# Six weight conversions in place, and at other places of the slot loop, in a fused attention, expert and MLP kernel

## The chip, the cores and the metric

One core of one Trainium2 chip runs the whole program. The metric is the device time of one execution in microseconds (us).

## What is computed

Three layers follow one another. The reference, cut to its arithmetic:

```python
def phi(x):                                       # q, k, v: (4, 8, 576, 64)
    proj = einsum('bhsd,df->bhsf', x, w_phi)      # 64 -> 128 features
    proj = proj - max(abs(proj), axis=-1)
    return concatenate([exp(proj), exp(-proj)])
num = phi(q) @ (phi(k).T @ v); den = phi(q) @ sum(phi(k)) + 1e-6
x = (num / den)                                   # -> (2304, 512)
e = argmax(normalised x @ normalised expert_emb.T / tau)      # one of 8 experts a token
x = gate * (relu(x @ w1[e]) @ w2[e])              # w1 512x1024, w2 1024x512
h = x @ w_in                                      # w_in 512x2048
out = (h / (1 + exp(-h))) @ w_out                 # w_out 2048x512
```

`w_in` and `w_out` come as 64-bit floats. The kernel reads them as pairs of 32-bit words, low word and high word, and makes 32-bit floats of them with bit operations.

## The kernel before

**The stages.** The attention runs first, batch by batch. The expert stage follows: the tokens are sorted by expert into slots of 128 tokens, and the loop over s handles slots 0 to 21. Last comes the MLP, in Strassen products. A 32-bit product is made of three matmuls of rounded parts (high by high, low by high, high by low), so each operand is split first: ScalarE (ACT) casts the high part, VectorE (DVE) subtracts to get the low part.

**One slot.** In slot s TensorE (PE) does `mm1(s, k)`, k = 0 to 3: 24 matmuls of tokens by w1. Then come four transposes of the next slot's tokens (`xturn(s + 1)`), `mm2(s - 1, i)`, i = 0 to 3: 24 matmuls of the hidden rows of the slot before by w2, and eight transposes of this slot's hidden rows (`hturn(s)`). Beside them run the splits: `split(s + 1, 1, k)` after `mm1(s, k)` and `split(s, 2, i)` after `mm2(s - 1, i)`. A split of a weight quarter is a cast on ACT (L848, raw to wh) and a subtraction on DVE (L849, raw and wh to wl). `halves` does the same for transposed tokens (xh, xl) and hidden rows (hh, hl), with its cast at L853 and its subtraction at L856. The third matmul of each product (L801) reads xl or hl.

**The weights.** `raw1` and `raw2` are two buffers each, one by parity of the slot. SyncE (SP) loads them at L812, in two parts: `load1(s + 3, (0,))` and `load1(s + 2, (1,))` in mm2 of slot s, `load2(s + 1, (0,))` and `load2(s, (1,))` at the head of slot s. A load waits until the splits that read the buffer's old contents are done, and it is left out where the expert does not change. All of SP's transfers are in one queue, in order.

**GpSimd (POOL)** issues its own transfers, in program order: a gather of tokens in each slot (L834), accumulating copies `add_weights` inside a scratch array of w_in blocks in DRAM (L194, by the list WHEN), the raw loads of the conversions (`cload`, L169), and the stores of their results (`keep_weights`, L182 to L186).

**The conversions.** The sixteen 128-wide blocks of w_in are converted one after another: ten in the attention, six, called conversion 0 to 5 here (i = CA to CA + 5 in the code), in the slots. Each is a shift of the low words (DVE; L209 for even i, L212 for odd), a multiplication of the high words by 2^-112 (ACT, L202), a shift-and-or (DVE, L217) and a sign xor (DVE, L219); an odd one adds its two column halves (DVE, L225). All work lies in one tile of the attention that is free by then, named x in the profile. It has 2560 words a partition: two raw halves of 1024 words for even and odd i, and one result buffer of 512 words that all six share (L943, words 2048 to 2560). `convert(s, n)` is called after each split of mm1 (n = k) and of mm2 (n = 4 + i), and the table HOOKS says at which of these places a conversion takes its next of five steps; the fifth stores it. Conversion 0 is in slots 4 and 5, 1 in 6 and 7, 2 in 7 and 8, 3 in 13 and 14, 4 in 14 and 15, 5 in 15 and 16. At the first step of conversion i the raw load of i + 1 is issued.

Of the kernel before, what the change touches and what calls it, by code (L numbers as in the profile page):

```python
# [66 lines left out]
def moe_kernel(ctx, tc, qk, v, w_phi, emb, tau, w1, w2, win, wout, out):  # L67
# [103 lines left out]
    def keep_weights(i, c, rw, dma=nc.sync):  # L171
# [25 lines left out]
    def narrow(rw, c, eng, i):  # L197
        minus = i < NJ and i % 2 == 0
        lo, hi = rw[:, :, 0], rw[:, :, 1]
        def scale():  # L200
            if eng is nc.scalar:
                nc.scalar.mul(out=c.bitcast(F32), in_=hi.bitcast(F32), mul=2.0 ** -112)  # L202
            else:
                eng.tensor_scalar(out=c.bitcast(F32), in0=hi.bitcast(F32), scalar1=2.0 ** -112, scalar2=None,
                                  op0=ALU.mult)

        def shift():
            if minus:
                nc.vector.tensor_scalar(out=lo, in0=lo, scalar1=29, scalar2=-2147483648, op0=ALU.logical_shift_right,  # L209
                                        op1=ALU.bitwise_or)  # L210
            else:
                nc.vector.tensor_scalar(out=lo, in0=lo, scalar1=29, scalar2=None, op0=ALU.logical_shift_right)  # L212

        for f in (shift, scale) if eng is nc.scalar else (scale, shift):
            f()
            yield
# [41 lines left out]
    def phase_all(ctx):  # L258
# [1364 lines left out]
```

## Time and profile before

| | |
|---|---|
| median of three runs | 923.42 us (923.1 to 924.58) |
| the profiled execution's own time | 923.77 us |
| its span in the trace | 922.1 us, so 1.67 us lie outside |
| busy in the span | PE 901.1, DVE 619.6, ACT 581.9, POOL 260.6 us |
| granted clock of PE | 1.00 in all windows that are shown (its upper level, 2.4 GHz) |
| slots 2 to 15 in the trace | 257.29 to 441.59 us |

The profile shows one execution. In a table by windows each line is one stretch of time, with the busy time of every engine in it. In a timeline each line is one instruction or a run of like instructions on one engine, with start and length; a bracket at its end says how long the engine sat idle before it and which instruction or transfer ended that. Names with an arrow are result and operands. SPq is a DMA issue on SP's queue.

### The profile page before, as it was taken

The numbers are of one execution on the slowest core, as the hardware profiler recorded it, in microseconds if no ns is written. First come the engines' busy times: TensorE is split into PE (matmuls) and PEld (weight loads), VectorE is DVE, ScalarE is ACT, GpSimd is POOL, SyncE is SP. The second block draws the span as 40 slices with busy tenths as digits, with TensorE's granted clock in tenths as the row PEclk, the third lists the DMA queues.
The fourth block names the chain that finished last, engine by engine and source line by source line (L and its number), as shares of the span: only waits on it lengthen the run. The fifth ranks groups of instructions, "written<-read, shape, count | busy, mean of one in ns | idle before, by whom it ended". The sixth has DMA issues, their size and how long they took to land. (4 is left out here: it accounts for less than half of the span.)

```text
span 922.1 us, 15645 instructions
## 1 busy us (share of the span) xinstructions
PE 901.1 (98%) x5567; PEld 786.3 (85%) x5567; DVE 619.6 (67%) x967; ACT 581.9 (63%) x948; POOL 260.6 (28%) x236
## 2 busy tenths in 40 slices
PE   8999999999999989999999999999999999999996
PEld 6999999988767767877888799999999888888885
DVE  7888888986798999969989857676756122222220
ACT  6877878745977869869888665343456344444331
POOL 6887877712221434313210020101000100000000
PEclk9999999999999999999999999999999999999999
DMA  6355363349496795793698585877776744444420
GB/s 181 107 152 180 93 178 97 99 126 359 160 256 194 237 240 170 277 322 110 180 335 305 196 289 180 248 248 231 242 255 210 202 115 125 115 114 115 116 67 23
DMA packets 136739, 171.69 MB, mean 186 GB/s; under 512 B 34664, under 2 KB 97768, under 8 KB 136656
## 3 DMA queue, kind: packets, MB, share of 16 engines
q1 hardware_dynamic: 124064, 144.06, 49.4%
q0 software_dynamic: 12512, 26.55, 10.8%
q8 instruction: 45, 0.74, 0.3%
q14 instruction: 38, 0.31, 0.1%
q10 hardware_dynamic: 80, 0.03, 0.0%
HBM read 170.87 MB, written 52.04 MB: 242 GB/s over the span
## 5 line engine op out<-in xcount | busy, mean ns | idle before, releaser
L849 DVE TENSOR_TENSOR wl<-raw,wh 128x1024 fp32r<-128x1024 f32 (+1 forms) x166 | 187.6, 1173 | 28.1 <-ACT wh L848 22.6
L848 ACT CAST wh<-raw 128x1024 fp32r<-128x1024 f32 (+1 forms) x166 | 161.2, 1033 | 22.2 <-PE ph L801 10.8
L1173 DVE TENSOR_TENSOR hlt<-gt,hlt 128x1024 fp32r<-128x1024 f32 x34 | 41.7, 1226 | 146.4 <-ACT hlt L1172 146.4
L1097 ACT COPY ht<-puA 128x288 f32<-128x288 f32 x128 | 50.9, 400 | 91.9 <-PE puA L801 78.9
L800 PE MATMUL po<-wob,hlt 128*128 128x512 f32 x272 | 108.6, 399 | 0.0
L799 PE MATMUL po<-wob,hlt 128*128 128x512 f32 x272 | 107.2, 394 | 0.0
L801 PE MATMUL po<-wob,hlt 128*128 128x512 f32 x272 | 106.6, 392 | 0.0
L435 POOL TENSOR_TENSOR kl<-ke,kh 128x640 fp32r<-128x640 f32 x52 | 84.0, 1636 | 31.0 <-issue 23.1
L1193 ACT COPY os<-po 128x512 f32<-128x512 f32 x17 | 10.0, 587 | 108.0 <-PE po L801 108.0
L485 PE MATMUL pnx<-kv,qp 128*128 128x73 f32 x640 | 76.6, 275 | 0.0
L485 PEld LDWEIGHTS pnx<-kv,qp 128*128 128x128 f32 x640 | 74.1, 192 | 0.1
L1194 POOL DMA_INDIRECT out<-os,oidx x18 | 17.5, 974 | 179.1 <-ACT os L1193 168.6
L799 PE MATMUL ph<-wh,xh 128*128 128x512 f32 x166 | 67.1, 404 | 0.0
L801 PE MATMUL ph<-wh,xl 128*128 128x512 f32 x166 | 65.3, 394 | 0.9 <-DVE xl L856 0.9
L800 PE MATMUL ph<-wl,xh 128*128 128x512 f32 x166 | 64.8, 390 | 0.0
L396 DVE TENSOR_REDUCE m<-pqk 128x10 f32<-128x1280 f32 x32 | 47.5, 1486 | 24.5 <-PE pqk L390 24.5
L1104 DVE TENSOR_TENSOR ht<-puC,ht 128x288 f32<-128x288 f32 x64 | 29.1, 454 | 51.4 <-PE puC L801 44.6
L799 PEld LDWEIGHTS po<-wob,hlt 128*128 128x128 f32 x272 | 51.1, 188 | 13.1
L420 ACT ACTIVATE ke<-d 128x640 f32<-128x640 f32 x52 | 38.3, 737 | 37.0 <-DVE d L397 37.0
L801 PEld LDWEIGHTS po<-wob,hlt 128*128 128x128 f32 x272 | 51.1, 188 | 12.3
L800 PEld LDWEIGHTS po<-wob,hlt 128*128 128x128 f32 x272 | 51.1, 188 | 11.8
L390 PE MATMUL pqk<-wbd,zh 128*128 128x256 f32 (+1 forms) x320 | 59.5, 285 | 0.8 <-DVE d L397 0.6
(403 smaller groups left out, 2438.3 us busy)
## 6 DMA issues: line engine op xcount, KB each, us to landing
raw<-w SPq DMA_DIRECT2D x44, 1536.0 KB
raw<-w SPq DMA_DIRECT2D x44, 512.0 KB
hd<-ht SPq DMA_DIRECT2D x124, 144.0 KB
gt<-hd SPq DMA_DIRECT2D x15, 1024.0 KB
z<-qk SPq DMA_DIRECT2D x32, 288.0 KB
wo<-wout SPq DMA_DIRECT2D x16, 512.0 KB
yd<-ys SPq DMA_DIRECT2D x23, 256.0 KB
raw<-win SPq DMA_DIRECT2D x10, 512.0 KB
```

The lines of the kernel that those rows point to most:

```text
L390: nc.tensor.matmul(out=pqk[0:r, c * 256:(c + 1) * 256], lhsT=z[:, c * P:c * P + r], rhs=wbd[:, j].rearrange("p h f -> p (h f)"), start=(i ...
L396: nc.vector.tensor_reduce(out=m, in_=pv, axis=AX.X, op=ALU.max, apply_absolute_value=True)
L420: nc.scalar.activation(out=ke, in_=kd, func=AF.Exp, scale=1.0 - 2.0 * s)
L435: nc.gpsimd.tensor_tensor(out=kl[:, :, s, :], in0=st.pop(("ke", g, s)), in1=kh[:, :, s, :].bitcast(F32), op=ALU.subtract)
L485: nc.tensor.matmul(out=pn[:, c, 0:73], lhsT=qp[:, s, c * P:(c + 1) * P], rhs=kv[:, s, 0:73], start=(s == 0), stop=(s == 1))
L799: nc.tensor.matmul(out=o, lhsT=ah, rhs=bh, start=first, stop=False, skip_group_check=more)
L800: nc.tensor.matmul(out=o, lhsT=ah, rhs=bl, start=False, stop=False, skip_group_check=more)
L801: nc.tensor.matmul(out=o, lhsT=al, rhs=bh, start=False, stop=last, skip_group_check=more)
L848: nc.scalar.copy(out=hi[:, 0:n], in_=sl[:, 0:n])
L849: nc.vector.tensor_tensor(out=lo[:, 0:n], in0=sl[:, 0:n], in1=hi[:, 0:n].bitcast(F32), op=ALU.subtract)
L1097: nc.scalar.copy(out=htile(u, at), in_=BK[u, "A"])
L1173: nc.vector.tensor_tensor(out=lo, in0=g, in1=hi.bitcast(F32), op=ALU.subtract)
```

## The change

A conversion writes its result back into its own raw half, and the shared buffer is gone. The order of the operations changes with that: shift of the low words, sign xor into the low words, multiplication of the high words in place, then shift-and-or into words 0 to 512 of the half; an odd conversion adds its halves into words 512 to 768 of the same half in that same step. So there are four steps, and loads and stores have tables of their own. The steps are in slots 2 (conversion 0), 7 and 8 (1), 9 (2), 10 (3), 14 (4) and 15 (5). The number of instructions on each engine and the transfers are the same as before; the conversions in the attention and those of w_out keep their operations.

```diff
+    def narrow_in_place(flat, i):
+        rw = flat.rearrange("p (f t) -> p f t", t=2)
+        lo, hi = rw[:, :, 0], rw[:, :, 1]
+        shift(lo, i)
+        yield
+        nc.vector.scalar_tensor_tensor(out=lo, in0=hi, scalar=-2147483648, in1=lo, op0=ALU.bitwise_and,
+                                       op1=ALU.bitwise_xor)
+        yield
+        nc.scalar.mul(out=hi.bitcast(F32), in_=hi.bitcast(F32), mul=2.0 ** -112)
+        yield
+        c = flat[:, 0:512]
+        nc.vector.scalar_tensor_tensor(out=c, in0=hi, scalar=3, in1=lo, op0=ALU.logical_shift_left, op1=ALU.bitwise_or)
+        if i % 2:
             a, b = c.bitcast(F32)[:, 0:256], c.bitcast(F32)[:, 256:512]
-            both = rw.rearrange("p f t -> p (f t)")[:, 0:256].bitcast(F32)
-            nc.vector.tensor_tensor(out=both, in0=a, in1=b, op=ALU.add)
+            nc.vector.tensor_tensor(out=flat[:, 512:768].bitcast(F32), in0=a, in1=b, op=ALU.add)
...
         def cload(i):
             scr = st[B - 1][1].rearrange("p c f -> p (c f)")
-            o = i % 2 * 1024
-            J[i] = [scr[:, o:o + 1024].bitcast(I32).rearrange("p (f t) -> p f t", t=2),
-                    scr[:, 2048:2560].bitcast(I32)]
-            fetch_raw(i, J[i][0], nc.gpsimd)
+            flat = scr[:, i % 2 * 1024:i % 2 * 1024 + 1024].bitcast(I32)
+            J[i] = [flat[:, 0:512], flat[:, 512:768], narrow_in_place(flat, i)]
+            fetch_raw(i, flat.rearrange("p (f t) -> p f t", t=2), nc.gpsimd)
...
-        HOOKS = [(s, n) for s, hs in {4: (1, 5), 5: (1, 5, 7), 6: (1, 3, 5, 7), 7: (1, 3, 5, 7), 8: (1, 3),
-                                      13: (1, 3, 5, 7), 14: (1, 3, 5, 7), 15: (1, 3, 5, 7), 16: (1, 3, 5)}.items()
-                 for n in hs]
-        assert len(HOOKS) == 5 * (NJ - CA)
+        LOADS = {(3, 5): 2, (8, 7): 3, (13, 5): 4, (13, 7): 5}
+        STORES = {(3, 1): 0, (8, 3): 1, (13, 1): 2, (13, 3): 3, (15, 1): 4, (16, 1): 5}
+        STEPS = [(2, (1, 3, 5, 7)), (7, (1, 5, 7)), (8, (1,))] + [(s, (1, 3, 5, 7)) for s in (9, 10, 14, 15)]
+        STEPS = [(s, n) for s, ns in STEPS for n in ns]
```

On ACT, the piece of slot 7 with the multiplication of a conversion, before (conversion 2), with the semaphores that each row waits for:

```order
L848 CAST wh_4356<-raw_1_159 128x1024 [waits DMAHW7_49,DVE_49,PE_49]
L848 CAST wh_4386<-raw_1_159 128x1024 [waits DVE_49,PE_49]
L202 ACTIVATE x<-x 128x512 [waits DMASW1_49,DMASW4_49,DMASW0_49,DVE_49]
L848 CAST wh_4397<-raw_1_159 128x1024 [waits PE_49,Activation_49]
L848 CAST wh_4405<-raw_1_159 128x512 [waits DMAHW5_49,PE_49,Activation_49]
L853 CAST hh<-ht_4413 128x512 [waits PE_49,Activation_49]
```

And the same place now, where the multiplication (L223) is that of conversion 1; L852 and L857 are the casts that were L848 and L853:

```order
L852 CAST wh_4347<-raw_1_159 128x1024 [waits DMAHW7_49,DVE_49,PE_49]
L852 CAST wh_4377<-raw_1_159 128x1024 [waits DVE_49,PE_49]
L852 CAST wh_4388<-raw_1_159 128x1024 [waits DVE_49,PE_49]
L852 CAST wh_4396<-raw_1_159 128x512 [waits DMAHW5_49,DVE_49,PE_49]
L223 ACTIVATE x<-x 128x512 [waits DMASW4_49,DVE_49]
L857 CAST hh<-ht_4404 128x512 [waits PE_49,Activation_49]
```

The multiplication moved behind two casts, and it waits for one semaphore of POOL's transfers (DMASW) where it waited for three.

On DVE, the tail of slot 8 and slot 9 up to the second subtraction of hidden rows, now; L853 and L860 are the subtractions that were L849 and L856, and L198, L220 and L226 are the shift, xor and shift-and-or of conversion 2:

```order
L860 TENSOR_TENSOR hl<-ht_4592,hh 128x384
...
L198 TENSOR_SCALAR x<-x 128x512
L853 TENSOR_TENSOR wl_4636<-raw_0_2785,wh_4635 128x1024
L220 SCALAR_TENSOR_TENSOR x<-x 128x512
L860 TENSOR_TENSOR xl<-pxt,xh 128x512
...
L226 SCALAR_TENSOR_TENSOR x<-x 128x512
L860 TENSOR_TENSOR hl<-ht_4737,hh 128x512
L860 TENSOR_TENSOR hl<-ht_4744,hh 128x384
```

Before, DVE had nothing but splits and halves in slots 9 and 10; the same three operations, and an addition, stand in slot 10 for conversion 3.

On POOL, from the gathers of slots 9 to 13 to the next but one, before:

```order
L834 DMA xg<-xd,gidx 128x512 x5
L194 DMA sscr_68<-sscr_68 128x256
L194 DMA sscr_69<-sscr_69 128x256
L194 DMA sscr_70<-sscr_70 128x256
L194 DMA sscr_71<-sscr_71 128x256
L169 DMA x<-win 128x4x256
L834 DMA xg<-xd,gidx 128x512
L194 DMA sscr_72<-sscr_72 128x3x256
```

And now, where L838 is the gather, L193 the accumulating copy, and L181 to L185 are stores:

```order
L838 DMA xg<-xd,gidx 128x512 x5
L193 DMA sscr_68<-sscr_68 128x256
L193 DMA sscr_69<-sscr_69 128x256
L193 DMA sscr_70<-sscr_70 128x256
L193 DMA sscr_71<-sscr_71 128x256
L185 DMA sscr_73<-x 128x512
L181 DMA sscr_73<-x 128x256
L182 DMA sscr_73<-x 128x256
L183 DMA sscr_73<-x 128x3x256
L169 DMA x<-win 128x4x256 x2
L838 DMA xg<-xd,gidx 128x512
L193 DMA sscr_72<-sscr_72 128x3x256
```

The four stores of conversions 2 and 3 and one more raw load came in between the accumulating copies and the next gather.

## Rows read from the trace of the kernel before

**Rows 1.** The page's busy times by engine, whole span.
```profile
PE 901.1 (98%) x5567; PEld 786.3 (85%) x5567; DVE 619.6 (67%) x967; ACT 581.9 (63%) x948; POOL 260.6 (28%) x236
```

**Rows 2.** Windows by slot: 2, 7, 8, 9, 10, 11, 13, 14; busy us (instructions), last: clock, DMA share, GB/s.
```profile
257.29:271.00 13.71, 13.24 (x60) 9.41 (x58) 13.43 (x25) 9.34 (x15) 1.66 (x2) 1.00 1.15 286
...
323.58:338.05 14.47, 12.70 (x62) 9.96 (x61) 14.30 (x26) 9.27 (x14) 4.45 (x5) 1.00 1.16 273
338.05:353.05 15.00, 13.62 (x83) 10.42 (x81) 13.60 (x17) 11.36 (x17) 4.58 (x5) 1.00 0.59 170
353.05:365.48 12.43, 12.43 (x62) 10.04 (x61) 12.40 (x15) 11.57 (x18) 7.42 (x3) 1.00 0.42 116
365.48:377.91 12.43, 12.43 (x62) 10.04 (x61) 12.43 (x14) 10.84 (x16) 1.94 (x1) 1.00 0.58 218
377.91:390.35 12.44, 12.44 (x63) 10.05 (x61) 10.85 (x12) 10.86 (x16) 5.49 (x6) 1.00 0.98 354
...
402.78:416.01 13.23, 13.01 (x63) 9.99 (x61) 6.50 (x10) 8.12 (x14) 0.00 (x0) 1.00 0.87 285
416.01:429.16 13.15, 12.70 (x62) 9.96 (x61) 13.15 (x16) 13.15 (x19) 2.09 (x3) 1.00 0.31 102
```

**Rows 3.** Timeline of PE: waits inside the slots 7, 8 and 14; start, us, instruction.
```profile
331.96 0.50 PE L801 MATMUL py<-wh,hl 128*128 128x512 f32 x1 [1.77 <-DVE hl L856]
...
346.41 0.51 PE L801 MATMUL po<-wh,hl 128*128 128x512 f32 x1 [1.33 <-DVE hl L856]
...
423.07 0.50 PE L801 MATMUL po<-wh,hl 128*128 128x512 f32 x1 [0.45 <-DVE hl L856]
```

**Rows 4.** Timeline of DVE, slots 5 to 8: operations of conversions, and halves.
```profile
307.45 1.51 DVE L217 SCALAR_TENSOR_TENSOR x<-x 128x512 int32<-128x512 int32 x1
...
330.62 0.69 DVE L219 SCALAR_TENSOR_TENSOR x<-x 128x512 int32<-128x512 int32 x1
331.22 1.15 DVE L856 TENSOR_TENSOR hl<-ht,hh 128x512 fp32r<-128x512 f32 x2
...
343.32 1.83 DVE L849 TENSOR_TENSOR wl<-raw,wh 128x1024 fp32r<-128x1024 f32 x2 [1.40 <-ACT wh L848]
```

**Rows 5.** Timeline of ACT, slots 7 and 8: its two long waits.
```profile
328.21 0.62 ACT L848 CAST wh<-raw 128x512 fp32r<-128x512 f32 x1 [4.73 <-DVE al L751]
...
341.69 0.66 ACT L202 ACTIVATE x<-x 128x512 f32<-128x512 f32 x1 [4.21 <-DMA sscr<-x]
```

**Rows 6.** Groups by line and form, whole span: busy us, mean ns, idle before.
```profile
L219 DVE SCALAR_TENSOR_TENSOR x<-x 128x512 int32<-128x512 int32 x6 | 4.1, 686 | 0.0
L212 DVE TENSOR_SCALAR x<-x 128x512 int32<-128x512 int32 x3 | 1.4, 478 | 0.0
L225 DVE TENSOR_TENSOR x<-x 128x256 f32<-128x256 f32 x3 | 1.3, 424 | 0.0
...
L202 ACT ACTIVATE x<-x 128x512 f32<-128x512 f32 x6 | 4.2, 702 | 8.7 <-DMA sscr<-x 4.2 <-DVE x L212 2.6 <-DVE hl L856 1.8
```

**Rows 7.** Timelines of DVE and PE, slot 10: hidden rows made, and first used.
```profile
368.47 1.15 DVE L856 TENSOR_TENSOR hl<-ht,hh 128x512 fp32r<-128x512 f32 x2
...
371.93 0.39 PE L801 MATMUL po<-wh,hl 128*128 128x512 f32 x1
```

**Rows 8.** Timelines of POOL, SP and ACT, slots 11 to 13.
```profile
385.43 3.56 POOL L194 DMA_DIRECT2D sscr<-sscr  x4
387.68 2.16 POOL L169 DMA_DIRECT2D x<-win  x1
...
391.29 0.38 SPq L812 DMA_DIRECT2D raw<-w  x1
...
407.89 0.62 ACT L848 CAST wh<-raw 128x512 fp32r<-128x512 f32 x1 [6.20 <-PE ph L801]
```

**Rows 9.** Windows of 2 us in slots 10 and 12, columns as in the windows by slot.
```profile
376.00:378.00 2.00, 2.00 (x13) 1.39 (x13) 2.00 (x2) 1.59 (x3) 0.00 (x0) 1.00 1.03 414
...
394.00:396.00 2.00, 2.00 (x11) 1.60 (x10) 1.73 (x3) 1.69 (x3) 0.00 (x0) 1.00 1.12 268
```

More of the change, by code (lines that the diff above doesn't have):

```diff
@@ L169, in fetch_raw, with keep_weights @@
         q.dma_start(out=dst, in_=src.bitcast(I32))
-    def keep_weights(i, c, rw, dma=nc.sync):
+    def keep_weights(i, c, both, dma=nc.sync):
         half, j = divmod(i, NJ)
@@ L180, in keep_weights @@
         elif odd:
-            both = rw.rearrange("p f t -> p (f t)")[:, 0:256].bitcast(F32)
             dma.dma_start(out=sscr[q][:, 6, :], in_=c[:, 0:256])
             dma.dma_start(out=sscr[q][:, 2, :], in_=c[:, 256:512])
-            dma.dma_start(out=sscr[q][:, 3:6, :], in_=both.unsqueeze(1).to_broadcast([P, 3, 256]))
+            dma.dma_start(out=sscr[q][:, 3:6, :], in_=both.bitcast(F32).unsqueeze(1).to_broadcast([P, 3, 256]))
         else:
@@ L195, in add_weights, with shift, narrow @@
                             accum_op=ALU.add)
-    def narrow(rw, c, eng, i):
-        minus = i < NJ and i % 2 == 0
-        lo, hi = rw[:, :, 0], rw[:, :, 1]
[L200 to L216, printed above, removed]
+    def shift(lo, i):
+        if i < NJ and i % 2 == 0:
+            nc.vector.tensor_scalar(out=lo, in0=lo, scalar1=29, scalar2=-2147483648, op0=ALU.logical_shift_right,
+                                    op1=ALU.bitwise_or)
+        else:
+            nc.vector.tensor_scalar(out=lo, in0=lo, scalar1=29, scalar2=None, op0=ALU.logical_shift_right)
+    def narrow(rw, c, i):
+        lo, hi = rw[:, :, 0], rw[:, :, 1]
+        nc.vector.tensor_scalar(out=c.bitcast(F32), in0=hi.bitcast(F32), scalar1=2.0 ** -112, scalar2=None,
+                                op0=ALU.mult)
+        yield
+        shift(lo, i)
+        yield
         nc.vector.scalar_tensor_tensor(out=c, in0=c, scalar=3, in1=lo, op0=ALU.logical_shift_left, op1=ALU.bitwise_or)
@@ L242, in work @@
             c = self.done(i)
-            yield from narrow(self.h[i], c, nc.vector, i)
-            self.h[i] = c, self.h[i]
+            yield from narrow(self.h[i], c, i)
+            self.h[i] = c, None
         def store(self, i):
@@ L1128, in oload @@
             t = pools["ul"].tile([P, 2048], F32, tag="ws", name="wo", bufs=2)
-            J[NJ + j] = [t[:, 0:1024].bitcast(I32).rearrange("p (f t) -> p f t", t=2), t[:, 1024:1536].bitcast(I32)]
-            fetch_raw(NJ + j, J[NJ + j][0])
+            rw, c = t[:, 0:1024].bitcast(I32).rearrange("p (f t) -> p f t", t=2), t[:, 1024:1536].bitcast(I32)
+            J[NJ + j] = [c, None, narrow(rw, c, NJ + j)]
+            fetch_raw(NJ + j, rw)
         WO = {}
```

27 lines of the change are left out of this document (11 added, 16 removed).

## The prediction

> **What bounds the kernel now.** I read the page's busy times first. PE is busy 901.1 of 922.1 us [rows 1], so a change in DVE or ACT work counts only where PE waits. The change touches slots 2 to 16, so I read the windows by slot next [rows 2]. Slots 9, 10 and 11 take 12.43 or 12.44 us with PE busy throughout: that is the price of a slot in which nothing waits. Against it slot 7 is 14.47 - 12.43 = 2.04 us too long. Slot 8 is too, but part of it is 20 small matmuls of the token sorting (83 instructions against 62). What is left of it is its idle time, 15.00 - 13.62 = 1.38 us, and some 0.27 us that slots 7 and 14 also show in busy time after a wait (12.70 against 12.43), together 1.65 us. Slot 13 is 0.80 and slot 14 0.72 us too long.
>
> The timeline of PE shows who ends these waits: three times it is the low part of the hidden rows, hl, from DVE [rows 3]. So DVE or what DVE waits for sets the end in slots 7, 8 and 14, and I read DVE and ACT around them.
>
> In slot 7 DVE has no idle time to speak of (14.30 of 14.47 us busy), and operations of conversions stand ahead of the hl that PE waits for. One L217 took 1.51 us, and L219 runs directly ahead of the hl at 331.22 [rows 4]. In slot 8 it is ACT: the multiplication L202 of conversion 2 sits 4.21 us until a store from the shared result buffer lands [rows 5]. The casts behind it are late, DVE idles 1.40 us for them [rows 4], and hl is late by 1.33 [rows 3]. In slot 14 conversion 3 has operations on DVE ahead of hl, and DVE is full (13.15 of 13.15).
>
> Slot 13 differs. ACT's cast of the last w2 quarter waits 6.20 us, until 407.89 [rows 8]. The row names PE as releaser, but the matmul it names was long done. What the cast needed is the second part of the w2 load that SP issued at 391.29: weights come late there. The DMA share is about 1 in that stretch, at 414 GB/s when loads are alone and at 268 when POOL's copies run beside them [rows 9].
>
> **The change, part by part.** *The shared buffer goes.* In slot 7 the multiplication waits for one POOL transfer where it waited for three, and it is conversion 1's, whose raw load has long landed. The 4.21 us of ACT and the 1.40 us of DVE go.
>
> *DVE work ahead of the hl of slot 7.* One L217 of 1.51 us, one L219, one shift, and another L217 and L219 stood between slots 5 and 7, by [rows 4, 6] 1.51 + 0.69 + 0.48 + 0.69 + 0.69 = 4.06 us. None of it is there now, and the gap is 1.77 us. Next in line is the cast of 328.21 [rows 5], a late weight. It ends at 328.83. PE's gap began at 331.96 - 1.77 = 330.19 [rows 3], so 1.36 us are left for the cast and the first subtraction of the hidden rows (0.69, the mean of L219 on as many elements), which is just enough. So slot 7 loses its 2.04. In slot 8 conversion 1 still has a shift, an xor and a shift-and-or with an addition around hl and the next xl. I keep 0.2 of the 1.65 for that. Slots 7 and 8 together: 2.04 + 1.65 - 0.2 = 3.5 us less.
>
> What the 1.51 us of L217 stands for matters here: it ran beside POOL's multiplication for the gates, the other five took 0.69. The Trainium skill says, on its page "SBUF — State Buffer", section "SBUF: two separate sides", that a DVE operation with two inputs in SBUF and a GpSimd operation that reads SBUF lock each other out for the whole instruction. The trace agrees with it in these 1.51 us. By that rule the split that now stands in L217's place would wait as long, and the 4.06 would be 3.2; the gap of 1.77 would go either way.
>
> *Conversion 0 into slot 2.* DVE has 13.43 of 13.71 us busy there [rows 2] and gets a shift and two longer operations, 0.48 + 0.69 + 0.69 = 1.86 us. The bounds are nothing and 1.86. The same work leaves slots 4 and 5, where DVE is busy as well, so it is a shift in time and no addition. I take nothing. A loss there would be taken back by the wait in slot 13, below.
>
> *Conversions 2 and 3 into slots 9 and 10.* They add 1.86 and, with an addition, 1.86 + 0.42 = 2.28 us to slots in which DVE is busy 12.40 and 12.43 of 12.43 [rows 2]. Does PE then wait? In slot 10 the first hl was ready at 368.47 + 0.69 = 369.16 and used at 371.93 [rows 7], 2.77 us ahead. With PE 3.5 us earlier DVE has to be 0.73 earlier there. By then it has lost 1.51 + 0.69 of conversion 0, 1.86 of conversion 2 and 1.40 of idle time, 5.46, and got conversion 2 back, 1.86. That leaves 3.6, or 1.8 if the late weight of slot 7 opens an idle stretch of 1.8. Either is enough, and no wait arises. But at the end of slot 10 DVE is ahead of its old time only by 5.46 - 4.14 = 1.3 us, while PE is ahead by 3.5.
>
> *What that does to the weights.* SP's loads wait for DVE's splits to free the buffers. Slot 11 leaves DVE 12.44 - 10.85 = 1.59 us to catch up, so the load of 391.29 [rows 8] is issued about 1.3 + 1.6 = 2.9, say 3.0 us earlier; not more than 3.5. At the same time POOL's stream grows. Behind its four copies at 385.43 came one raw load of 512 KB. Now there come the stores of conversion 2 (256 KB) and 3 (128, 128 and 384 KB) and two raw loads, 1,408 KB or 1.44 MB more ahead of the landing. At the 268 GB/s of [rows 9] that is 5.4 us if the loads wait for all of it. It is nothing if it fits beside them. I take 2.5, about half, since each side keeps moving while the other does. Let L be the shift of that landing. It is -3.0 + 2.5 = -0.5 us, with ends at -3.5 and 5.4 - 3.0 = +2.4.
>
> *Slot 13.* PE comes 3.5 us earlier to a landing that moves by L. So slot 13 grows by 3.5 + L = 3.0 us. This is the wait that takes the place of the removed ones.
>
> *Slot 14.* Conversion 3 is gone from it. Of conversion 4 a shift and an xor stand ahead of hl, about 0.7 less than now. Of its 0.72 I count 0.6 as gone.
>
> *Operations themselves.* Their number is the same. The multiplication now writes every second word. No row shows such a write on ACT. It reads so already at 702 ns [rows 6]; at twice that, six times 0.7 us would lie on ACT, which has idle time in every slot but 14. I take nothing.
>
> **Sum**: -3.5 + 3.0 - 0.6 = -1.1 us, that is L - 0.6. Against the profiled execution's own 923.77 it gives 922.67. That execution lies 0.35 above the median of 923.42, against which the forecast is **922.3 us**.
>
> **Rivals.** *The loads come in time.* If the 1.44 MB fit beside the loads and these are issued 3.5 us earlier, L is -3.5, slot 13 stays as it is, and the time is 923.42 - 3.5 - 0.6 = 919.3. For it speaks that slots 8 and 9 have DMA shares of 0.59 and 0.42 [rows 2], so there is room further ahead. Against it, the share is about 1 where POOL issues.
>
> *Slower: POOL's stream takes its turns from the loads.* If all 1.44 MB are served ahead of the w2 part (5.4 us) and the load is issued only 2.5 us earlier, L is +2.9 and the time 923.42 + 2.9 - 0.6 = 925.7. It is slower by over 0.2% from L = +2.45 on, a landing near 410. For it speaks the fall from 414 to 268 GB/s beside POOL's copies [rows 9]. Against it, stores issued right behind the copies are served partly before that load is issued. The Trainium skill says on "DMA: Bandwidth & Descriptors", section "Queues, rings and completion order", that each DMA engine goes round the queues that have work, packet by packet. By that rule POOL's stream would hold its share to its end; the trace agrees as far as the two rates go.
>
> *The change doesn't take the wait away.* The multiplication of slot 7 still waits for DVE's xor ahead of it. If that wait were as long as the old one, slot 8 would keep its 1.65. PE would reach slot 13 by 1.85 instead of 3.5 us earlier, and as long as the landing decides, the time is the same 922.3. Only if the loads were early would it show, as 921.0.
>
> **How the numbers follow.** I give the forecast 0.56, with L between -2 and +1, its own range 920.8 to 923.8. The loads in time have 0.18, POOL's stream 0.18, and a wait that stays 0.08. A measurement of this kernel tells 0.2% from no change, 1.85 us. Of the forecast, L below -1.25 is faster by more than that, which I put at 0.22; the other 0.34 are within. Faster is 0.18 + 0.22 = 0.40, same 0.34 + 0.08 = 0.42, slower 0.18. The range takes in the loads in time, a little below their 919.3, and the slower rival up to L = +2.4, that is 919.2 to 925.2.
>
> **What would show it.** In the changed profile slots 7 and 8 should have no PE wait over 0.3 us for hl, and the multiplication no wait for a store. Slot 13 should be about 16.2 us long, with the cast of the last w2 quarter near 407.4, and slot 14 near 12.5. I am wrong if slot 13 stays near 13.2 (the loads were early), if that cast is after 410, or if PE waits for hl or xl in slots 2 to 5, 9 or 10.

## The result, and the profile after

The change makes the kernel slower: 930.8 us median of four runs (928.5 to 930.92) against 923.52, a ratio of 1.0071 with a 95% interval of 1.0053 to 1.0089 (it is worked out from all runs and need not be the ratio of the two medians). The forecast was 922.3, with a range up to 925.2. The profiled execution took 930.92 us with a span of 929.2.

The busy times of the page barely move [rows 1]; PE gets 1.6 us more, in a span that is 7.1 longer:

```profile
PE 902.7 (97%) x5567; PEld 787.3 (85%) x5567; DVE 619.0 (67%) x967; ACT 581.7 (63%) x948; POOL 267.9 (29%) x236
```

Here are the windows by slot of the changed kernel (slots 7, 8, 11, 13, 14, 15 and 18), columns as in [rows 2]:

```profile
323.89:343.34 19.45, 14.99 (x62) 11.57 (x61) 13.36 (x23) 9.99 (x15) 0.00 (x0) 0.82 0.79 217
343.34:356.31 12.97, 12.97 (x82) 10.54 (x81) 12.45 (x17) 10.65 (x17) 1.63 (x3) 1.00 0.09 32
...
381.18:393.62 12.44, 12.44 (x63) 10.05 (x61) 12.41 (x15) 10.91 (x16) 6.01 (x8) 1.00 1.04 375
...
406.05:420.51 14.46, 12.98 (x62) 9.99 (x61) 9.78 (x11) 9.61 (x15) 5.88 (x6) 1.00 1.07 348
420.51:435.07 14.56, 12.99 (x62) 9.99 (x61) 10.68 (x13) 10.31 (x16) 0.63 (x1) 1.00 0.52 137
435.07:447.71 12.64, 12.64 (x62) 9.97 (x61) 12.64 (x16) 12.64 (x20) 5.87 (x3) 1.00 0.11 43
...
472.58:487.22 14.64, 13.54 (x70) 10.79 (x69) 11.77 (x15) 11.65 (x18) 1.94 (x1) 1.00 0.98 373
```

Against [rows 2], slot 8 is 2.03 us shorter, without a wait. But slot 7 is 4.98 us longer, slot 13 is 1.23 longer and slot 14 is 1.41 longer. Slot 18 took 13.48 before and is 1.16 longer. The rest of the 7.1 us is some tenths in slots 2, 6 and 15.

PE's timeline shows what PE waits for in slots 7, 13 and 14. In slots 7 and 14 it was hl from DVE before [rows 3]. In all three it is now hh from ACT, at the head of mm2:

```profile
334.51 0.80 PE L803 MATMUL py<-wh,hh 128*128 128x512 f32 x1 [4.46 <-ACT hh L857]
...
413.58 0.50 PE L803 MATMUL py<-wh,hh 128*128 128x512 f32 x1 [1.37 <-ACT hh L857]
...
428.14 0.50 PE L803 MATMUL po<-wh,hh 128*128 128x512 f32 x1 [1.47 <-ACT hh L857]
```

On ACT the cast of hh stands behind the cast of the last w2 quarter, and that one waits for its weights each time:

```profile
333.35 0.62 ACT L852 CAST wh<-raw 128x512 fp32r<-128x512 f32 x1 [10.55 <-DMA raw<-w]
...
412.42 0.62 ACT L852 CAST wh<-raw 128x512 fp32r<-128x512 f32 x1 [4.85 <-DMA raw<-w]
...
426.98 0.62 ACT L852 CAST wh<-raw 128x512 fp32r<-128x512 f32 x1 [4.25 <-DMA raw<-w]
```

In slot 7 the cast starts at 333.35 where it started at 328.21 [rows 5]. SP issues the load at the same time as before, 316.34 against 316.61 (first line changed, second line before):

```profile
316.34 0.87 SPq L816 DMA_DIRECT2D raw<-w  x1
```
```profile
316.61 0.38 SPq L812 DMA_DIRECT2D raw<-w  x1
```

So the load itself takes longer: 17.0 us from issue to cast, where it took 11.6. What runs beside it is in POOL's timeline. Before the change:

```profile
315.00 0.62 POOL L186 DMA_DIRECT2D sscr<-x  x1 [6.58 <-DVE x L219]
315.93 1.41 POOL L834 DMA_INDIRECT xg<-xd,gidx  x1 [0.30 <-issue]
317.34 3.93 POOL L194 DMA_DIRECT2D sscr<-sscr  x3
```

And after:

```profile
309.51 1.80 POOL L838 DMA_INDIRECT xg<-xd,gidx  x1 [0.15 <-PE py L865]
311.30 3.94 POOL L193 DMA_DIRECT2D sscr<-sscr  x3
315.55 1.59 POOL L838 DMA_INDIRECT xg<-xd,gidx  x1 [0.30 <-issue]
317.09 2.65 POOL L193 DMA_DIRECT2D sscr<-sscr  x2
```

POOL used to sit 6.58 us at conversion 0's store, waiting for DVE's xor. That wait held back everything behind it in POOL's order. The store is in slot 3 now, so the three accumulating copies of slot 6 go out at 311.30 instead of 317.34, and the two of slot 7 at 317.09 (323.41 before). These five copies, and a smaller one of slot 8 at 321.10, are under way while the last 512 KB of that w2 are loaded. (The raw load of conversion 2, at 319.71 before, has left for slot 3.)

The DMA view of the stretch from the load's issue to the cast shows what the DMA engines moved in it. q0 is POOL's queue (POOL's transfers of the whole run add up to its 26.5 MB), q1 holds SP's; the columns are packets, MB, and the share of the engines' time that the packets took. Before the change:

```profile
q1 hardware_dynamic: 1194, 2.35, 64.3%
q0 software_dynamic: 720, 0.95, 40.1%
```

And after:

```profile
q0 software_dynamic: 1852, 2.04, 69.8%
q1 hardware_dynamic: 1216, 2.40, 42.1%
```

SP's queue moved about the same, POOL's more than twice as much.

The wait then costs a second time. Windows of 1 us in slot 7 of the changed kernel (column before the last two: granted clock):

```profile
332.00:333.00 1.00, 0.00 (x0) 0.00 (x0) 0.00 (x0) 0.00 (x0) 0.00 (x0) 0.79 1.14 287
333.00:334.00 1.00, 0.00 (x0) 0.00 (x0) 0.00 (x0) 0.65 (x2) 0.00 (x0) 0.50 1.13 315
...
339.00:340.00 1.00, 1.00 (x5) 0.82 (x4) 1.00 (x2) 1.00 (x3) 0.00 (x0) 0.79 0.44 168
340.00:341.00 1.00, 1.00 (x6) 0.80 (x5) 1.00 (x3) 1.00 (x2) 0.00 (x0) 1.00 0.26 94
```

While PE idled, its clock fell to the lower level, 1.2 GHz, and it came back near 340. Of the 19.45 - 12.43 = 7.02 us that slot 7 is too long, 4.46 are the wait and 2.56 are matmuls at the lower clock and their restart.

### The profile page after: what moved, and what is told of

Its sections match the earlier page's. It is cut to its first block, busy times and chain, and to the rows that moved or that the text cites. A ratio compares the mean times of both kernels' runs of the same rounds, so it can differ in the third digit from the quotient of the medians.

```text
span 929.2 us, 15649 instructions
## 1 busy us (share of the span) xinstructions
PE 902.7 (97%) x5567; PEld 787.3 (85%) x5567; DVE 619.0 (67%) x967; ACT 581.7 (63%) x948; POOL 267.9 (29%) x236
## 5 line engine op out<-in xcount | busy, mean ns | idle before, releaser
L853 DVE TENSOR_TENSOR wl<-raw,wh 128x1024 fp32r<-128x1024 f32 (+1 forms) x166 | 187.4, 1175 | 36.6 <-ACT wh L852 31.6
L852 ACT CAST wh<-raw 128x1024 fp32r<-128x1024 f32 (+1 forms) x166 | 161.1, 1034 | 33.9 <-DMA raw<-w 24.8
L1004 POOL DMA_INDIRECT yt<-yd,yidx x13 | 15.4, 1185 | 160.1 <-PE pt L1021 159.8
```

The lines of the kernel that those rows point to most:

```text
L852: nc.scalar.copy(out=hi[:, 0:n], in_=sl[:, 0:n])
L853: nc.vector.tensor_tensor(out=lo[:, 0:n], in0=sl[:, 0:n], in1=hi[:, 0:n].bitcast(F32), op=ALU.subtract)
```

## The experiments

Theory A says that weights come late because POOL's transfers, no longer held back, run beside SP's loads. The first runs set it against theories that blame the in-place steps or DVE's work. The kernel before was measured beside each group of runs, so each ratio stands for itself.

**The copies of slots 6 to 8 in slots 9 to 11.**

```diff
-    WHEN = [1, 1, 2, 2, 4, 6, 6, 6, 7, 7, 8, 13, 13, 13, 13, 14, 15, 15, 16, 17, 18]
+    WHEN = [1, 1, 2, 2, 4, 9, 9, 10, 10, 11, 11, 13, 13, 13, 13, 14, 15, 15, 16, 17, 18]
```

> The changed kernel, with the five accumulating copies of slots 6 and 7 (and the one of slot 8) issued in slots 9 to 11 instead. Theory A: in the changed kernel conversion 0's store no longer holds POOL back in slot 5 (6.58 us before), so these copies run beside the load of the last w2 part of slot 7, which lands near 333 instead of 328; PE waits 4.46 us for it, and its clock then falls to the lower level. By A the wait in slot 7 falls below 0.6 us here, the clock stays at 1.00 in slot 7, and slot 7 shrinks from 19.4 to 12.4 to 13 us; some of this is taken back in slots 13 and 14, so the time is 924 to 927.5. Theory B: the wait comes from the in-place steps themselves (their order on ACT and DVE, or conversion 0's work in slot 2); then the wait stays over 3 us and the time within 1.5 of the change's 930.8.

Measured: 930.05 us against 921.24, ratio 1.0075 (1.0047 to 1.0103). Windows of slots 7, 8 and 13, and the first matmul of mm2 in slot 13:

```profile
325.61:338.04 12.43, 12.43 (x62) 10.04 (x61) 12.26 (x23) 10.75 (x16) 0.00 (x0) 1.00 0.29 100
338.04:351.00 12.96, 12.96 (x82) 10.53 (x81) 12.44 (x15) 9.04 (x14) 0.77 (x2) 1.00 0.06 22
...
401.39:424.37 22.98, 14.50 (x63) 11.24 (x61) 12.46 (x13) 13.37 (x19) 7.48 (x6) 0.78 1.03 324
```
```profile
416.05 0.80 PE L803 MATMUL py<-wh,hh 128*128 128x512 f32 x1 [8.48 <-ACT hh L857]
```

Slot 7 is down to the clean 12.43 us and slot 8 to 12.96, as A says. But the time did not follow: slot 13 now waits 8.48 us. Taking back "some of this" was far too mild, so the second half of the expectation failed.

**Conversion 0 early, and nothing else,** in the kernel before:

```diff
-        HOOKS = [(s, n) for s, hs in {4: (1, 5), 5: (1, 5, 7), 6: (1, 3, 5, 7), 7: (1, 3, 5, 7), 8: (1, 3),
+        HOOKS = [(s, n) for s, hs in {2: (1, 3, 5, 7), 3: (1,), 6: (1, 3, 5, 7), 7: (1, 3, 5, 7), 8: (1, 3),
```

> The kernel before, shared buffer and all, with one edit: conversion 0's steps in slot 2 and its store in slot 3, where the change has them. Theory A: POOL is free earlier, its copies of slots 6 and 7 move beside the w2 load, and the old kernel gets a wait of 3 to 5 us in slot 7 and a lower clock after it; time 927 to 931. Theory B: nothing new in slot 7; the time stays within 1.5 of the 923.5 before, or a little under it since DVE has less to do in slots 4 and 5.

Measured: 926.13 us, ratio 1.0051 (1.0033 to 1.0068). PE's wait in slot 7:

```profile
334.94 0.80 PE L799 MATMUL py<-wh,hh 128*128 128x512 f32 x1 [4.92 <-ACT hh L853]
```

The old kernel, with its shared buffer, gets the changed kernel's wait from this one move (the time lies a little under the range that A gave). So the in-place steps do not make the wait. That conversion 0's work in slot 2 does not make it either is shown by the run before, which has that work and no wait, and by the next one, which has the wait without that work. Together they rule out theory B.

**Only the store later in POOL's order.** Even the steps stay here; the store of conversion 0 is issued behind slot 6's gather and three copies.

```diff
-        HOOKS = [(s, n) for s, hs in {4: (1, 5), 5: (1, 5, 7), 6: (1, 3, 5, 7), 7: (1, 3, 5, 7), 8: (1, 3),
+        HOOKS = [(s, n) for s, hs in {4: (1, 5), 5: (1, 5), 6: (0, 1, 3, 5, 7), 7: (1, 3, 5, 7), 8: (1, 3),
```

> The kernel before with a single transfer moved in POOL's order: the store of conversion 0 behind the gather and the three copies of slot 6 instead of ahead of them; all steps of conversions stay. Theory A: POOL no longer waits 6.58 us for conversion 0's xor before it issues these three copies, so they are issued near 311 instead of 317, beside the w2 load of slot 7; its last part lands later and PE's wait in slot 7 grows from 1.77 to 3 us or more. If only all five copies together do it (the two of slot 7 still come behind the store and the raw load), it grows by less than 1 us.

Measured: 925.55 us, ratio 1.0034 (1.0020 to 1.0048). POOL and PE:

```profile
309.75 3.96 POOL L194 DMA_DIRECT2D sscr<-sscr  x3
314.94 0.62 POOL L186 DMA_DIRECT2D sscr<-x  x1 [1.23 <-DVE x L219]
```
```profile
324.39 0.82 PE L901 MATMUL ht<-ident,hs 128*128 128x128 f32 x5 [1.51 <-ACT hs L889]
...
335.08 0.79 PE L799 MATMUL py<-wh,hh 128*128 128x512 f32 x1 [3.28 <-ACT hh L853]
```

One transfer moved in a queue, and what stood behind it is issued earlier: the copies by 7.6 us, the raw load of conversion 2 by 4.2 (315.55 instead of 319.71). The load of slot 7, issued at 316.55, is cast at 333.93, and PE waits 3.28 us. A second wait of 1.51 appears in slot 6 that was not expected. The wait of POOL at that store had been a brake that kept these transfers away from the load. Windows of slots 7 and 8:

```profile
325.36:344.77 19.41, 15.90 (x61) 11.69 (x60) 18.17 (x29) 14.58 (x21) 1.95 (x3) 0.82 0.72 204
344.77:357.76 12.99, 12.99 (x82) 10.54 (x81) 12.99 (x16) 11.13 (x17) 8.02 (x6) 1.00 0.44 121
```

Slot 7 is as long as in the changed kernel. The time rises less, since a late PE finds no wait in slots 8, 13 and 14 (12.99, 12.43 and 12.44 us). In slot 8 that holds although the shared buffer is still in use.

**In place at the old places.** The changed kernel with the HOOKS, loads and stores of the kernel before.

```diff
...
-        STEPS = [(2, (1, 3, 5, 7)), (7, (1, 5, 7)), (8, (1,))] + [(s, (1, 3, 5, 7)) for s in (9, 10, 14, 15)]
...
+        HOOKS = [(s, n) for s, hs in {4: (1, 5), 5: (1, 5, 7), 6: (1, 3, 5, 7), 7: (1, 3, 5, 7), 8: (1, 3),
+                                      13: (1, 3, 5, 7), 14: (1, 3, 5, 7), 15: (1, 3, 5, 7), 16: (1, 3, 5)}.items()
...
```

> Conversions in place as in the change, at the old places (slots 4 to 8 and 13 to 16), with loads and stores at theirs. Theory A: slot 7 keeps about the wait of before (1.8 us), slot 8 loses its 1.33 us wait for the store from the shared buffer, and slot 13 takes back most of that; time 921.5 to 923.5. Theory B: slot 7 waits over 3 us, time 927 or more.

Measured: 922.7 us against 921.24 in the medians, ratio 1.0001 (0.9986 to 1.0017): no difference. Slot 7 keeps a wait of 1.95 us for hl, slot 8 has none, and slot 13 takes that back with 1.20:

```profile
332.18 0.50 PE L805 MATMUL py<-wh,hl 128*128 128x512 f32 x1 [1.95 <-DVE hl L860]
...
408.75 0.50 PE L803 MATMUL py<-wh,hh 128*128 128x512 f32 x1 [1.20 <-ACT hh L857]
```

Here is slot 7's load in these runs, with the MB that each queue moved between its issue and its cast:

| kernel | issue to cast, us | POOL's queue | SP's queue |
|---|---|---|---|
| copies later | 8.73 | 0.26 | 2.35 |
| before | 11.60 | 0.95 | 2.35 |
| in place, old places | 11.66 | 1.03 | 2.35 |
| changed | 17.01 | 2.04 | 2.40 |
| only the store later | 17.38 | 2.49 | 2.49 |
| only conversion 0 early | 17.50 | 2.36 | 2.40 |

SP's queue has nearly the same to move each time, and the load takes longer where POOL's queue moves more. A longer stretch takes in more transfers, but the rate of POOL's queue rises too, from 30 GB/s in the first line over 82 to 120 in the changed kernel.

**Stores and raw loads spread out.**

```diff
-        LOADS = {(3, 5): 2, (8, 7): 3, (13, 5): 4, (13, 7): 5}
-        STORES = {(3, 1): 0, (8, 3): 1, (13, 1): 2, (13, 3): 3, (15, 1): 4, (16, 1): 5}
+        LOADS = {(3, 5): 2, (8, 7): 3, (10, 7): 4, (14, 1): 5}
+        STORES = {(3, 1): 0, (8, 3): 1, (10, 1): 2, (11, 1): 3, (15, 1): 4, (16, 1): 5}
```

> The changed kernel, with the stores of conversions 2 and 3 in slots 10 and 11 instead of 13, and the raw loads of 4 and 5 in slots 10 and 14 instead of 13. Theory A: the new waits of slots 13 and 14 (1.37 and 1.47 us) are weights that land late beside these transfers, so both fall below 0.5 us; slot 7 stays as in the change (about 4.4 us); time 927 to 928.5. Theory C: the waits of slots 13 and 14 come from DVE's conversion work in slots 9 and 10, or from the four copies of slot 13 alone; then they stay over 1 us each and the time within 1 of 930.8.

Measured: 931.47 us, ratio 1.0105 (1.0082 to 1.0128), and a miss for A as I had put it: slot 14's wait is gone, but slot 13 waits 4.53 us. Theory C, as put, had the time right and slot 14 wrong. POOL's order may explain a part:

```profile
385.70 0.55 POOL L181 DMA_DIRECT2D sscr<-x  x1 [6.03 <-ACT wh L852]
...
391.09 3.58 POOL L193 DMA_DIRECT2D sscr<-sscr  x4
```

POOL waits 6.03 us at conversion 3's store, and the four copies behind it go out at 391.09 (388.73 in the changed kernel). SP also issues the load later, as the table below shows. No run separates the two.

**POOL's transfers out of slot 13.** This starts from the run with the copies later. The copies, stores and raw loads of slot 13 go to slots 14 and 16; DVE's conversions 2 and 3 stay in slots 9 and 10. Conversions 4 and 5 and the later copies go to later slots too.

```diff
-    WHEN = [1, 1, 2, 2, 4, 9, 9, 10, 10, 11, 11, 13, 13, 13, 13, 14, 15, 15, 16, 17, 18]
+    WHEN = [1, 1, 2, 2, 4, 9, 9, 10, 10, 11, 11, 16, 16, 16, 16, 17, 17, 17, 18, 18, 18]
...
-        LOADS = {(3, 5): 2, (8, 7): 3, (13, 5): 4, (13, 7): 5}
-        STORES = {(3, 1): 0, (8, 3): 1, (13, 1): 2, (13, 3): 3, (15, 1): 4, (16, 1): 5}
-        STEPS = [(2, (1, 3, 5, 7)), (7, (1, 5, 7)), (8, (1,))] + [(s, (1, 3, 5, 7)) for s in (9, 10, 14, 15)]
+        LOADS = {(3, 5): 2, (8, 7): 3, (14, 3): 4, (14, 7): 5}
+        STORES = {(3, 1): 0, (8, 3): 1, (14, 1): 2, (14, 5): 3, (16, 1): 4, (17, 1): 5}
+        STEPS = [(2, (1, 3, 5, 7)), (7, (1, 5, 7)), (8, (1,))] + [(s, (1, 3, 5, 7)) for s in (9, 10, 15, 16)]
```

> The run with the copies issued later (wait of 8.48 us in slot 13), with one more step: everything POOL issues in slot 13 except the gathers (four copies, the stores of conversions 2 and 3, two raw loads) is issued in slots 14 to 16 instead, conversions 4 and 5 a slot later; the DVE work of conversions 2 and 3 stays in slots 9 and 10. Theory A1: the late landing of slot 13 is made by POOL's transfers beside the load; then the wait in slot 13 goes (below 0.5 us) and the time is 3 to 5 us below the kernel before. Theory A2: it is made by DVE's work in slots 9 and 10, which frees the weight buffers about 3 us later; then a wait of 2 us or more stays in slot 13, and the time is above the kernel before less 2 us.

Measured: 921.8 us against 922.32, ratio 0.9998 (0.9982 to 1.0014). Slots 13 and 18:

```profile
399.63:412.06 12.43, 12.43 (x62) 10.04 (x61) 9.93 (x12) 9.77 (x16) 2.61 (x4) 1.00 0.93 324
...
461.80:479.12 17.32, 14.30 (x70) 11.55 (x69) 12.14 (x15) 12.12 (x18) 3.60 (x3) 0.95 1.04 343
```

The wait of slot 13 is gone, with DVE's work still in slots 9 and 10, as A1 says. Of POOL's work only a gather (393.63) and one store of 256 KB (396.60) are issued while that load is under way. The gain in time that A1 forecast did not come. It went to slot 18, now 17.32 us long, where ACT waits 3.95 us for weights (472.65). That the moved copies delay them is likely and not shown by this run; the last run below, which issues them earlier, has slot 18 clean.

**The four copies back in slot 13,** alone:

```diff
-    WHEN = [1, 1, 2, 2, 4, 9, 9, 10, 10, 11, 11, 16, 16, 16, 16, 17, 17, 17, 18, 18, 18]
+    WHEN = [1, 1, 2, 2, 4, 9, 9, 10, 10, 11, 11, 13, 13, 13, 13, 17, 17, 17, 18, 18, 18]
```

> The run with POOL's transfers out of slot 13 (no wait there), with only the four accumulating copies put back into slot 13; stores and raw loads stay in 14. It splits the wait of 8.48 us between the copies and the rest. If bytes count, the copies are 4 x 128 KB against 1,920 KB of stores and loads, so they make 1 to 3 us of wait in slot 13. If the copies are what slows the loads (they move few bytes for the time they take), 4 us or more. If neither alone is enough, none. Slots 7 and 8 as there (12.4 and 13.0 us).

Measured: a wait of 1.03 us in slot 13, at the low end of what bytes would make. The copies alone add 2.4 us from issue to cast (14.28 against 11.88 in the table below). The larger part of the 22.0 us of the run with the copies later comes only with the stores and raw loads beside them. (The time, 926.65 us, ratio 1.0036, 1.0017 to 1.0055, has slot 18's wait in it.)

**DVE's work of conversions 2 and 3 cut,** in the run with the copies later; two blocks of w_in are stored after their shift alone.

```diff
         shift(lo, i)
+        if i - CA in (2, 3):
+            return
         yield
```

> The run with the copies of slots 6 and 7 issued later (wait of 8.48 us in slot 13), with conversions 2 and 3 cut down to their shift: xor, multiplication, shift-and-or and addition are left out, so two blocks of w_in are not converted, and DVE has about 3.2 us less in slots 9 and 10. All transfers stay. Theory A1 (POOL's transfers beside the load are the cause): the wait in slot 13 stays over 5 us, shorter only by what the load is issued earlier. Theory A2 (DVE's work frees the buffers late): the load of the last w2 part is issued about 3 us earlier against slot 12's start, and the wait falls by 3 us or more, to 5.5 or less. If both have to meet, it falls below 2.

Measured: 929.41 us, ratio 1.0073 (1.0039 to 1.0108). The wait is 8.22 us instead of 8.48:

```profile
414.48 0.80 PE L805 MATMUL py<-wh,hh 128*128 128x512 f32 x1 [8.22 <-ACT hh L859]
```

Beside the same transfers, about 3.2 us less DVE work brought the issue 0.69 us forward and gave 0.26 us. So A2, as it was put, does not hold: DVE's conversion work makes neither the wait nor most of the late issue.

**One sum for slot 13 in all these runs.** I took from each trace how long after the start of slot 12 SP issues the load of the last w2 part, and how long it is from there to the cast. The two together, less 17.4 us (the value that fits the kernel before), give PE's wait. This only keeps the books, since slot 12 takes 12.43 us in all of them; it shows which of the two terms grew:

| kernel | issued after start of slot 12 | issue to cast | sum - 17.4 | PE's wait for hh |
|---|---|---|---|---|
| before | 0.94 | 16.60 | 0.14 | 0.11 |
| changed | 2.47 | 16.33 | 1.40 | 1.37 |
| in place, old places | 0.94 | 17.69 | 1.23 | 1.20 |
| stores spread | 3.35 | 18.62 | 4.57 | 4.53 |
| copies later | 3.91 | 22.03 | 8.54 | 8.48 |
| the same, less DVE | 3.22 | 22.44 | 8.26 | 8.22 |
| four copies back in 13 | 4.19 | 14.28 | 1.07 | 1.03 |
| POOL out of 13 | 4.27 | 11.88 | none | none |

From issue to cast it is 11.9 us with POOL almost quiet and 22 in the run with the copies later. (A load of 1.5 MB for the next slot is issued 0.74 us ahead of it in SP's own queue, so this is not the time of 512 KB alone.) But POOL's list does not decide alone. The changed kernel has the same four copies, stores and raw loads there, and its load took 16.33 us, no longer than before. Between issue and cast POOL's queue moved 1.66 MB before, 2.26 in the changed kernel and 3.05 in the run with the copies later, and SP's own queue 3.74, 3.85 and 5.01. What makes this difference isn't settled.

The issue is 1.5 to 3.3 us later against PE in all kernels with conversions 2 and 3 in slots 9 and 10, and that alone costs nothing (last line). Beside a slow load it does cost: in the run with the copies later the sum is 8.4 us above that of the kernel before, 2.97 from the later issue and 5.43 from the longer way to the cast. What makes the issue late in each of them isn't settled: cutting DVE's work brought it from 3.91 to 3.22 only, and in that run casts also waited for earlier loads.

**What in-place work is worth.** Two kernels have the same places and lists, with POOL quiet in slots 11 to 13, one in place and one with the shared buffer.

```diff
-    WHEN = [1, 1, 2, 2, 4, 6, 6, 6, 7, 7, 8, 13, 13, 13, 13, 14, 15, 15, 16, 17, 18]
+    WHEN = [1, 1, 2, 2, 4, 6, 6, 6, 7, 7, 8, 9, 9, 10, 10, 16, 16, 16, 17, 18, 18]
...
-                                      13: (1, 3, 5, 7), 14: (1, 3, 5, 7), 15: (1, 3, 5, 7), 16: (1, 3, 5)}.items()
+                                      13: (7,), 14: (1, 3, 5, 7), 15: (1, 3, 5, 7), 16: (1, 3, 5, 7), 17: (1, 3)}.items()
...
```

> Conversions 0 to 2 in place at their old places, the four copies of slot 13 in slots 9 and 10, conversion 3 to 5 and their loads half a slot to a slot later, later copies from slot 16 on, so that POOL issues only gathers in slots 11 to 13. Slot 7 keeps its wait of about 1.9 us, slot 8 has none, slot 13 none: 2 to 3.5 us below the kernel before. If in-place work buys nothing, it equals the next run.

> The same places and lists as the run before it, with the shared result buffer of the kernel before. Slot 8 keeps its wait of 1.3 us for the store, slot 13 has none; 0.8 to 1.5 us below the kernel before, and 1.2 to 2 us above the in-place run with the same places.

Measured: in place 919.9 us, ratio 0.9979 (0.9965 to 0.9993). Shared 921.52, ratio 0.9994 (0.9984 to 1.0003). The difference of the medians is 1.6 us. The two intervals overlap, so the times alone do not show it; slot 8 does, 13.20 us against 14.90 (in place first):

```profile
338.20:351.40 13.20, 13.20 (x83) 10.54 (x81) 12.71 (x16) 9.31 (x15) 3.41 (x4) 1.00 0.61 175
```
```profile
337.90:352.80 14.90, 13.57 (x81) 10.39 (x80) 13.57 (x17) 11.31 (x17) 4.45 (x5) 1.00 0.58 170
```

**Two tries for a faster kernel.** The first puts only conversion 2 in slot 9, conversions 3 to 5 in slots 14 to 16, and ten copies in slots 15 to 18.

```diff
...
+    WHEN = [1, 1, 2, 2, 4, 9, 9, 9, 10, 10, 10, 15, 15, 15, 16, 16, 16, 17, 17, 18, 18]
...
+        LOADS = {(3, 5): 2, (8, 7): 3, (10, 3): 4, (15, 3): 5}
+        STORES = {(3, 1): 0, (8, 3): 1, (10, 1): 2, (15, 1): 3, (16, 1): 4, (17, 1): 5}
+        STEPS = [(2, (1, 3, 5, 7)), (7, (1, 5, 7)), (8, (1,))] + [(s, (1, 3, 5, 7)) for s in (9, 14, 15, 16)]
```

> In place, conversion 0 in slot 2, 1 in slots 7 and 8, 2 in slot 9 as in the change; conversion 3 in slot 14, 4 in 15, 5 in 16; the six copies of slots 6 to 8 in slots 9 and 10, the other ten from slot 15 on, and POOL issues only gathers in slots 11 to 14. If both the DVE work ahead of slot 13 and POOL's transfers matter, no wait above 0.6 us is left in slots 6 to 14: slots 7, 8, 13 and 14 lose 2.0, 1.6, 0.8 and up to 0.7 us against the kernel before, 4 to 5 us together. If POOL's ten later copies meet other loads, slots 17 to 19 show new waits.

Measured: 922.52 us against 922.32, ratio 1.0002 (0.9987 to 1.0017), no gain where 4 to 5 us were expected. Slots 7, 8, 13 and 14 are clean, but slot 12 waits 1.21 us for a gather that POOL issued late and slot 18 waits 3.12. The second try keeps POOL out of slot 13 and issues the copies before slot 18's loads:

```diff
-    WHEN = [1, 1, 2, 2, 4, 6, 6, 6, 7, 7, 8, 13, 13, 13, 13, 14, 15, 15, 16, 17, 18]
+    WHEN = [1, 1, 2, 2, 4, 9, 9, 10, 10, 11, 11, 15, 15, 15, 15, 15, 15, 16, 16, 17, 18]
...
+        LOADS = {(3, 5): 2, (8, 7): 3, (14, 3): 4, (14, 7): 5}
+        STORES = {(3, 1): 0, (8, 3): 1, (14, 1): 2, (14, 5): 3, (15, 5): 4, (16, 5): 5}
+        STEPS = [(2, (1, 3, 5, 7)), (7, (1, 5, 7)), (8, (1,)), (9, (1, 3, 5, 7)), (10, (1, 3, 5, 7)),
+                 (14, (5, 7)), (15, (1, 3, 5, 7)), (16, (1, 3))]
```

> In place, conversions 0 to 3 where the change has them, copies of slots 6 to 8 in slots 9 to 11, the stores of conversions 2 and 3 and the loads of 4 and 5 in slot 14, all later copies but two in slots 15 and 16, conversion 4 in slots 14 and 15, 5 in 15 and 16, so that slot 18's load meets what it met in the kernel before. Slots 7, 8, 13, 14 without waits (4.7 us less up to slot 18, as in the run with POOL's transfers out of 13) and no wait above 0.5 us in slot 18: 4 to 5 us below the kernel before. If slot 18 still waits for late weights, 0 to 2 us below.

Measured: 918.51 us against 922.71, ratio 0.9959 (0.9944 to 0.9973), faster than both kernels. Slots 7, 8, 13, 14 and 18:

```profile
323.58:336.01 12.43, 12.43 (x62) 10.04 (x61) 12.26 (x23) 10.84 (x16) 0.00 (x0) 1.00 0.33 107
336.01:348.98 12.97, 12.97 (x82) 10.53 (x81) 12.45 (x15) 9.07 (x14) 0.82 (x2) 1.00 0.06 22
...
399.30:411.73 12.43, 12.43 (x62) 10.04 (x61) 10.26 (x12) 10.31 (x15) 2.62 (x4) 1.00 0.99 352
411.73:424.16 12.43, 12.43 (x62) 10.04 (x61) 11.33 (x14) 11.09 (x17) 7.90 (x8) 1.00 0.87 202
...
461.46:474.78 13.32, 13.32 (x71) 10.87 (x69) 12.04 (x15) 11.77 (x18) 0.00 (x0) 1.00 1.04 396
```

## Why the prediction was wrong, step by step

*The shared buffer goes: right.* Slot 8 lost 2.03 us, where I had 1.65 less 0.2. That slot alone does not prove it, since PE comes 5 us late to it, and with only the store later slot 8 is clean with the shared buffer too. The two kernels with the same places prove it, 13.20 us against 14.90. The multiplication still waits in slot 8 for DVE's xor, 2.3 us, as the third rival had it, and PE doesn't feel it.

*"So slot 7 loses its 2.04": the step that failed.* The working took DVE's 4.06 us out and named the cast of 328.21 as next in line. It took that time for fixed. The load behind it lands 5 us later as soon as POOL is no longer stuck at conversion 0's store. Slot 7 came out 4.98 us longer instead of 2.04 shorter: 7.02 of the 8.2 us between the forecast change of -1.1 and the span's 7.1. A moved step counts in every queue that it is moved past. I priced POOL's stream in slot 13 and left it out in slots 5 to 7, where the change takes a transfer out of POOL's order. The two runs that move only conversion 0, or only its store, settle this. With the copies out of the way slot 7 is 12.43, so the 2.04 were there to be had. The split that stands in place of the L217 of 1.51 us was slowed beside POOL's multiplication: two splits took 3.18 us at 307.25, where two took 2.34 before at 310.63. It did not matter, since PE waited for the weights.

*Conversion 0 into slot 2 at nothing: right for DVE,* 0.1 us in slot 2. Its price was its store's place in POOL's queue.

*No wait in slots 9 and 10: right, with luck.* PE reaches slot 9 of the changed kernel 3.26 us late, where I had it 3.5 early. In the run with the copies later, where PE is early, slot 10 is clean, but slot 9 takes 13.09 us: PE waits 0.21 there for xl, behind conversion 1's last step and addition. In slot 11 of the changed kernel the first hl, ready at 385.64 + 0.68 = 386.32, still is ahead of its use, by 387.63 - 386.32 = 1.31 us:

```profile
385.64 1.15 DVE L860 TENSOR_TENSOR hl<-ht,hh 128x512 fp32r<-128x512 f32 x2
```
```profile
387.63 0.39 PE L805 MATMUL py<-wh,hl 128*128 128x512 f32 x1
```

*Slot 13: right mechanism, wrong size.* I wrote that PE would come early to a late landing, with L = -3.0 + 2.5. In the changed kernel the cast stands at 412.42, past the 410 that was to show me wrong, but the forecast wait can't be read there, since PE came 3.3 us late. The run with the copies later is the case that I had described (slots 7 and 8 clean, all else as changed), and there slot 13 waits 8.4 us longer than before, not 3.0. Both terms are off. SP issues the load 3.91 us after the start of slot 12, where 0.94 + 3.5 - 3.0 = 1.4 was forecast; that is 2.5 later. From issue to cast it takes 22.0 instead of 16.6 us, 5.4 more, where I took 2.5; that is another 2.9. The upper bound, 1.44 MB at the 268 GB/s of [rows 9], was 5.4 too, but that the two agree may be chance: SP's own queue moved 1.27 MB more in that (longer) stretch than before, that run's copies in slots 9 to 11 may have a share, and in the changed kernel the same stream made the load no longer. So 2.5 was too little for that run, and what would have been the right term stays open.

The Trainium skill's page "DMA: Bandwidth & Descriptors", section "Queues, rings and completion order", has each DMA engine go round its queues packet by packet. The traces agree with it as far as a load beside POOL's transfers is slower, in slot 7 8.73 us with 0.26 MB of POOL's beside it and 17.01 with 2.04; no run shows the order of packets. The rival that it stood beside had 0.18.

*Slot 14, 0.6 us less: wrong in the change.* Two raw loads go out at 404.36 and 406.88, near that slot's own w2 load, and slot 14 waits 1.47 us for its cast. It is clean, 12.43 or 12.44, where only one raw load goes out there (at 402.66 with the stores spread, 404.35 with POOL out of 13, 404.38 in the last run), but also in the run with the copies later, where both stay and PE comes late. No run changes the raw loads alone, so that they make the wait is likely and not shown.

*Slot 18* isn't in the prediction. ACT waits 2.03 us there for weights (481.51), where it waited 0.87 before (474.23); which transfers delay them is not shown.

*The operations themselves at nothing: right.* The multiplication in place takes 0.69 us (median of six), where it took 0.70.

*The rivals.* "The loads come in time" gave 919.3, 4.1 us under the kernel before. It did not happen here; the last run, which makes the loads come in time by other places for POOL's transfers, is 4.2 us under. "POOL's stream takes its turns from the loads" is the nearest to what happened, but in slot 7, where I had not looked for it. The lower clock, 2.56 us of slot 7, was in no case.

## What to carry to other kernels

A wait in an in-order queue may protect something: before you remove it, list what stands behind it and which urgent transfer those will run beside. Price transfers that share the DMA engines with an urgent load by what falls between its issue and its landing, and don't take half of a bound without a row for it: in slot 7, 2.04 MB of POOL's queue instead of 0.95 made the load 5.4 us longer. And when a step is moved, follow it through every queue at both ends, where it leaves as well as where it arrives.

## What the runs showed of the hardware that was not expected

- A load of the last w2 part takes 11.9 us from issue to cast with POOL almost quiet and 22.0 beside copies, stores and raw loads. The DMA share is about 1 in both, 0.93 to 1.08.
- POOL's queue took more of the DMA engines' time for its bytes than SP's: in slot 7 of the changed kernel 69.8% for 2.04 MB, where SP's queue took 42.1% for 2.40 MB.
- During a wait of 4.46 us PE's granted clock fell to 0.50 and was back at 1.00 near 340; slot 7 lost 2.56 us beyond the wait. With the 8.48 us wait it was 22.98 - 12.43 - 8.48 = 2.07, and in the run with only the store later, after waits of 1.51 and 3.28 us, 19.41 - 12.43 - 3.28 = 3.70. Waits of 1.37 and 1.47 us left the clock at 1.00.
- One of SP's own issues of a load took long beside POOL's stream: 3.98 us at 392.86 in the run with the copies later, where 0.38 is usual [rows 8]. It is part of the 22.0.

```profile
392.86 3.98 SPq L816 DMA_DIRECT2D raw<-w  x1
```
